# Attention, MLP and gated MLP in one kernel: keys and values in two runs a batch, the shared tile scored once, side work placed anew

## The chip, the cores and the metric

One core of one Trainium2 chip runs the whole kernel. The metric is the device time of one execution in microseconds (us). Everything is in float32; most products are taken as three matmuls over a high and a low part of each operand.

## The reference, cut to what matters

```python
# q, k, v: [8 batches, 8 heads, 576, 64]; phi: [8, 8, 576, 32]
a = phi - max(phi, axis=2); a = exp(a); a = a / (sum(a, axis=2) + 1e-9)
k_m = einsum('bhsm,bhsd->bhmd', a, k)        # 32 memory slots a head
v_m = einsum('bhsm,bhsd->bhmd', a, v)
s = q @ k_m.T / sqrt(64); s = exp(s - max(s)); attn = s / (sum(s) + 1e-9)
x = (attn @ v_m) laid out as [8, 576, 512]
x = x + relu(layer_norm(x) * g_ln @ w_ch1) @ w_ch2          # hidden width 2048
h = gelu(x @ w_in); u, w = halves of h                       # width 1024
out = x + (u * (w_sg @ layer_norm(w) + b_sg)) @ w_out       # w_sg: 576 x 576
```

## The kernel before, in words

Phase 1 is attention and the first MLP. The 8 batches go through it in 4 pairs of an even and an odd batch. A pair has 9 tiles of 128 rows; tile 4, the shared tile, holds the last 64 rows of the even batch and the first 64 of the odd one. Phase 2 is the gated MLP, after all of phase 1.

The MLP's first weight is folded with the values: per batch and per block of 512 hidden columns (fb, four of them), `pvw` = values x centred w_ch1 (16 matmuls, a "vw run", `make_vw`), and the hidden activations come out of the attention weights and `vw` directly: `ph` (line L541), then relu and its low part (`hh` on ACT, `hl` on DVE; `cr` for the 64 columns that belong to the shared tile), then `py` (L570 to L572) sums the second product. `ph` and `py` are the main work of PE (TensorE) in phase 1. A list of steps, one per block of columns and chunk of hidden units, sets their order.

All the rest is side work: for each batch `load_phi`, `prep_max`, `prep_exp`, `prep_sum` (slot weights; `pt`, `mb`, `ptsum` on PE), `load_kv` and `prep_kv` (`kvp`, sums of keys and values over the sequence), `prep_T` (`ptk`, transposed keys), `prep_vb`, and for each group of q tiles `lay_q` and `load_q` (q goes through DRAM, `q_d`), `t_q` (`qT`, a transpose on DVE), `t_scores` (`sc`), `t_norm`, `t_attn`, `t_x` (`px`) and `t_ln`. Each is entered with `at_time(time, ...)`. Times count in units in which a batch's main steps take 18; the list is sorted and the entries are emitted between main steps. `BASES` has the times of a batch's three groups of q tiles, `vw_at` those of the vw runs, and the times around keys and values follow from the batch's first group. A scheduler then orders each engine's instructions by their emission and by what they wait for, and an engine works through its order strictly. So an instruction that waits holds up all behind it on its engine. All loads and stores are issued by SP (L83), in its own order.

Keys and values in detail: a batch has 576 = 4 x 128 + 64 rows. From batch 1 on `prep_kv` runs three times a batch: 32 matmuls over the full chunks of heads 0 to 3, 16 over the 64 remaining rows of all heads (`phir`), 32 over the full chunks of heads 4 to 7. Tile `kv` has two buffers, of which a run takes two, and the remainder takes two of the same tag; so the loads of a run can start only when the run before has read its buffers. Every matmul of a run waits for all loads of the run. DVE then scales (`kvn`, L304) or scales and adds (L307).

Scores and vw runs first have DVE clear two columns of each of the two output buffers (L367, L483); all of a run's matmuls wait for both clears, so a run starts only once DVE has come to them in its order. These outputs, `kvp`, `ptk`, `px` and the small transposes share two PSUM buffers (`ps_a`).

Of the kernel before, what the change touches and what calls it, by code (L numbers as in the profile page):

```python
# [28 lines left out]
def fused_kernel(ctx: ExitStack, tc: tile.TileContext, q, k, v, phi, g1, w1, w2, w_in, g2, w_sg, b_sg, w_out, out):  # L29
# [5 lines left out]
    DM = H * D  # L35
# [26 lines left out]
    ones = const.tile([P, P], F32, name="ones")  # L62
    G.memset(ones, 1.0)
# [74 lines left out]
    def phase1():  # L138
# [32 lines left out]
        def load_phi(b, gs):  # L171
            if gs[0] == 0:
                st["phi", b] = (
                    at.tile([P, H, 4, NM], F32, tag="phi", name="phi"),
                    at.tile([REM, H, NM], F32, tag="phir", name="phir"),
                )
            ph, pr = st["phi", b]
            hs = slice(4 * gs[0], 4 * gs[-1] + 4)
            with behind_w2(b, 5):
                load(ph[:, hs], phi[b, hs, 0:4 * P, :].rearrange("h (p c) m -> p h c m", c=4))  # L180
                load(pr[:, hs], phi[b, hs, 4 * P:S, :].rearrange("h p m -> p h m"))

        def load_kv(b, g, part):
            n = 3 * g + part
# [5 lines left out]
            with behind_w2(b, 6 + n):  # L190
                ins = []
                for i, src in enumerate((k, v)):
                    if part < 2:
                        ld = load(
                            t[:, i],
                            src[b, hs, 0:4 * P, :].rearrange("h (p c) d -> p h c d", c=4)[:, :, 2 * part:2 * part + 2, :],
                        )
                    else:
                        ld = load(t[:REM, i, :, 0, :], src[b, hs, 4 * P:S, :].rearrange("h p d -> p h d"))
                    ins.append(ld.ins.name)  # L200
            st["kv", b, g, part] = t, ins

# [26 lines left out]
        def prep_max(b, gs):  # L229
# [13 lines left out]
            for g in range(n):  # L243
                V.tensor_scalar(dg[:, g, :], ident, mx[:, g:g + 1], None, op0=ALU.mult)
            st["dg", b] = dg

        def prep_exp(b, gs):
# [3 lines left out]
            PE.matmul(mb.rearrange("p h m -> p (h m)"), ones, st["dg", b].rearrange("p g n -> p (g n)"), start=True, stop=True)  # L251
            V.tensor_tensor(out=ph[:, hs], in0=ph[:, hs], in1=mb.unsqueeze(2).to_broadcast([P, 4 * n, 4, NM]), op=ALU.subtract)
            V.tensor_tensor(out=pr[:, hs], in0=pr[:, hs], in1=mb[:REM], op=ALU.subtract)
            A.activation(ph[:, hs], ph[:, hs], AF.Exp)
            A.activation(pr[:, hs], pr[:, hs], AF.Exp)

        def prep_sum(b):
# [5 lines left out]
            G.tensor_tensor(out=sm[:REM], in0=sm[:REM], in1=pr, op=ALU.add)  # L263
# [9 lines left out]
        def prep_kv(b, *parts):  # L273
            ph, pr = st["phi", b]
            if b or parts[0] == (0, 0):
                st["kvp", b] = ps_a.tile([P, 2, 2, D], F32, tag="a", name="kvp")
            if ("kvn", b) not in st:
                st["kvn", b], st["seen", b] = at.tile([P, 2, 2, D], F32, tag="kva", name="kvn"), set()
            kvp, kvn, seen = st["kvp", b], st["kvn", b], st["seen", b]
            kvs = {gp: st.pop(("kv", b, *gp)) for gp in parts}  # L280
            lands = [n for _, ins in kvs.values() for n in ins] if b else []
            for g in sorted({g for g, _ in parts}):
                cs = [c for g_, part in parts if g_ == g for c in range(2 * part, min(2 * part + 2, 5))]
                ts = {part: kvs[g, part][0] for g_, part in parts if g_ == g}
                for c in cs:
                    n = P if c < 4 else REM
                    for j in range(4):
                        h = 4 * g + j
                        mm = PE.matmul(  # L289
                            kvp[32 * j:32 * j + 32, :, g, :],  # L290
                            ph[:, h, c, :] if c < 4 else pr[:, h, :],
                            ts[c // 2][:n, :, j, c % 2, :],
                            start=(c == (cs[0] if b else 0)),
                            stop=(c == (cs[-1] if b else 4)),
                            skip_group_check=True,
                        )
                        for name in lands:
                            tc.add_manual_dep(mm.ins, name, ORDER, reason="all of the group together")
            if not b:
                return  # L300
            rs = st["rs", b]
            for g in sorted({g for g, _ in parts}):
                if g not in seen:
                    V.tensor_scalar(kvn[:, :, g, :], kvp[:, :, g, :], rs[:, g:g + 1], None, op0=ALU.mult)  # L304
                    seen.add(g)
                else:
                    V.scalar_tensor_tensor(  # L307
                        out=kvn[:, :, g, :], in0=kvp[:, :, g, :], scalar=rs[:, g:g + 1], in1=kvn[:, :, g, :], op0=ALU.mult, op1=ALU.add
                    )

        def prep_norm(b):
            kvp, kvn, rs = st["kvp", b], st["kvn", b], st["rs", b]
            for g in range(2):
                V.tensor_scalar(kvn[:, :, g, :], kvp[:, :, g, :], rs[:, g:g + 1], None, op0=ALU.mult)
# [48 lines left out]
        def t_scores(gr):  # L363
            w, b = gr["w"], gr["b"]
            kT, qT = st["kvT", b][0][:, 0, :], gr["qT"]
# [635 lines left out]
```

## Time and profile before

| what | us |
|---|---|
| three timed runs | 1247.18, 1250.12, 1248.4 |
| their median | 1248.4 |
| the profiled execution | 1248.95 |
| its span in the trace | 1247.1 |
| busy time of PE / DVE / ACT / POOL | 1190.5 / 708.1 / 467.1 / 399.0 |

The span is the trace's own extent; the profiled execution's time is 1.85 us more. The granted clock of TensorE is 0.99 of full speed over the span. Phase 1 ends and phase 2's main work begins at about 795 us. In the trace's timelines a row is a start, a length, the engine and line, the operation with its output and inputs, the number of instructions in it, and in brackets the idle time of the engine before it with what ended that; overlapping lengths of pipelined matmuls are normal, so what one costs is read from one start to the next.

### The profile page before, as it was taken

The page shows a single profiled execution, that of the slowest core. Times are in us where ns is not written, and L with a number is a line of the kernel's source. Part 1 is how long each engine was busy: PE and PEld are TensorE (multiplying, and loading weights), DVE is VectorE, ACT ScalarE, POOL GpSimd, SP SyncE. Part 2 cuts the span into 40 slices and gives each one's busy share as a digit, 9 for nine tenths or more (in the row PEclk, how much of TensorE's full clock was granted, in tenths as well). Part 3 has the DMA queues.
Part 4 walks back from the last instruction along what each step waited for, and adds up shares of the span by engine and source line. Part 5 has one row for each costly group of instructions (what it writes and reads, how often), then busy time and mean ns, then how long its engine had stood idle before and what let it go on. Part 6 is the DMA issues. An engine that isn't in the chain of part 4 may idle for free.

```text
span 1247.1 us, 21009 instructions
## 1 busy us (share of the span) xinstructions
PE 1190.5 (95%) x7711; PEld 990.4 (79%) x7711; DVE 708.1 (57%) x1699; ACT 467.1 (37%) x1067; POOL 399.0 (32%) x617
## 2 busy tenths in 40 slices
PE   5699799989999999999999989999999999999998
PEld 3377578877887878878877767789988988998997
DVE  2886564464645654655545566664467457547632
ACT  2665232223333333333323445433354354444430
POOL 2133211121111121111211233324486565657641
PEclk9899999999999999999999999999999999999999
DMA  9996761437515436426353254120141033013201
GB/s 204 266 261 190 215 176 35 145 73 201 119 52 169 109 81 188 94 65 174 89 140 94 68 169 134 51 79 26 51 126 52 1 117 112 1 59 103 77 18 68
DMA packets 204406, 138.85 MB, mean 111 GB/s; under 512 B 94992, under 2 KB 176016, under 8 KB 204304
## 3 DMA queue, kind: packets, MB, share of 16 engines
q1 hardware_dynamic: 204304, 137.51, 40.2%
q8 instruction: 61, 1.00, 0.3%
q14 instruction: 41, 0.34, 0.1%
HBM read 114.40 MB, written 31.33 MB: 117 GB/s over the span
## 4 chain that ended last, share of the span: by engine, by line
PE 79%; DMA 7%; DVE 6%; ACT 2%; issue 2%; SPq 2%; POOL 1%; DVEq 0%; POOLq 0%; ACTq 0%
PE ph L541 13%; PE pvs L910 10%; PE py L570 9%; PE py L571 8%; PE py L572 8%; PE pu L885 8%; PE po L933 8%; PE pv L815 8%; DMA raw<-in_moe_w_ch_dram 3%; PE pvw L487 2%; SPq L83 2%; DMA q<-q_d 2%; PE kvp L289 2%; DMA raw<-in_moe_w_in_dram 1%; DVE qT L358 1%
## 5 line engine op out<-in xcount | busy, mean ns | idle before, releaser
L541 PE MATMUL ph<-aTh,vw 128*128 128x320 f32 (+1 forms) x1024 | 246.3, 301 | 5.3 <-ACT vw L498 3.7
L570 PE MATMUL py<-whl,hh 128*128 128x512 f32 x512 | 206.9, 407 | 6.2 <-ACT hh L527 5.8
L571 PE MATMUL py<-whl,hh 128*128 128x512 f32 x512 | 203.2, 397 | 0.0
L541 PEld LDWEIGHTS ph<-aTh,vw 128*128 128x128 f32 x1024 | 178.4, 191 | 29.3 <-ACT vw L498 9.0
L572 PE MATMUL py<-whl,hl 128*128 128x512 f32 x512 | 183.5, 397 | 0.0
L527 ACT ACTIVATE hh<-ph 128x256 fp32r<-128x256 f32 x256 | 96.3, 384 | 169.3 <-PE ph L541 114.0
L528 DVE SCALAR_TENSOR_TENSOR hl<-ph,hh 128x256 fp32r<-128x256 f32 x256 | 106.1, 419 | 86.8 <-ACT hh L527 85.3
L541 PE MATMUL ph<-aTl,vw 128*128 128x320 f32 (+1 forms) x512 | 153.1, 300 | 0.0
L570 PEld LDWEIGHTS py<-whl,hh 128*128 128x128 f32 x512 | 97.1, 190 | 42.0 <-ACT hh L527 16.8
L910 PE MATMUL pvs<-wsh,vhl 128*128 128x288 f32 x576 | 121.4, 294 | 0.0
L571 PEld LDWEIGHTS py<-whl,hh 128*128 128x128 f32 x512 | 97.4, 190 | 20.9 <-issue 3.1
L885 PE MATMUL pu<-yTh,whl 128*128 128x288 f32 x512 | 111.3, 295 | 0.0
L541 PEld LDWEIGHTS ph<-aTl,vw 128*128 128x128 f32 x512 | 97.6, 191 | 9.8 <-issue 2.1
L572 PEld LDWEIGHTS py<-whl,hl 128*128 128x128 f32 x512 | 90.6, 189 | 12.6 <-issue 3.1
L910 PEld LDWEIGHTS pvs<-wsh,vhl 128*128 128x128 f32 x576 | 94.3, 188 | 0.5
L394 POOL TENSOR_TENSOR z<-z,r 128x512 f32<-128x512 f32 (+1 forms) x21 | 17.5, 833 | 233.6 <-DVE r L393 148.5
L815 PE MATMUL pv<-whl,yTh 128*128 128x512 f32 x288 | 90.9, 395 | 0.0
L933 PE MATMUL po<-whl,gh 128*128 128x512 f32 x288 | 90.3, 391 | 0.0
L885 PEld LDWEIGHTS pu<-yTh,whl 128*128 128x128 f32 x512 | 85.2, 188 | 1.0
L910 PE MATMUL pvs<-wsl,vhl 128*128 128x288 f32 x256 | 75.4, 295 | 0.0
L885 PE MATMUL pu<-yTl,whl 128*128 128x288 f32 x256 | 75.4, 295 | 0.0
L527 ACT ACTIVATE cr<-ph 128x64 fp32r<-128x64 f32 x128 | 28.3, 222 | 122.6 <-PE ph L541 122.4
(156 smaller groups left out, 2218.2 us busy)
## 6 DMA issues: line engine op xcount, KB each, us to landing
wc<-w_d SPq DMA_DIRECT2D x56, 512.0 KB, 5.0
y_d<-x SPq DMA_DIRECT2D x36, 256.0 KB, 2.6
yt<-y_d SPq DMA_DIRECT2D x36, 256.0 KB, 2.7
yr<-y_d SPq DMA_DIRECT2D x36, 256.0 KB, 2.9
kv<-in_k_dram SPq DMA_DIRECT2D x32, 256.0 KB, 4.4
kv<-in_v_dram SPq DMA_DIRECT2D x32, 256.0 KB, 4.5
raw<-in_moe_w_ch_dram SPq DMA_DIRECT2D x32, 256.0 KB, 8.2
raw<-in_moe_w_ch_dram SPq DMA_DIRECT2D x16, 512.0 KB, 7.2
```

Of the source, the lines that this page charges most:

```text
L83: return nc.sync.dma_start(out=out_ap, in_=in_ap)
L289: mm = PE.matmul(kvp[32 * j:32 * j + 32, :, g, :], ph[:, h, c, :] if c < 4 else pr[:, h, :], ts[c // 2][:n, :, j, c % 2, :], start=(c == ( ...
L527: A.activation(out_h, src, AF.Relu)
L528: return V.scalar_tensor_tensor(out=out_l, in0=src, scalar=0.0, in1=out_h.bitcast(F32), op0=ALU.max, op1=ALU.subtract)
L541: PE.matmul(ph, w_[:, ks], x[:, g, 0:w], start=(n == 0), stop=(n == 3 * HK - 1))
L570: PE.matmul(py, hh, wh, start=start, stop=False)
L571: PE.matmul(py, hh, wl, start=False, stop=False)
L572: PE.matmul(py, hl, wh, start=False, stop=stop)
L815: PE.matmul(pv, y[:, kc, cs], w, start=(n == 0), stop=(n == 3 * KC - 1))
L885: PE.matmul(pu, w[:, ds_], y[:, kc, cs], start=(n == 0), stop=(n == 3 * KC - 1))
L910: PE.matmul(pvs, v_, w_, start=(n == 0), stop=(n == len(ops) - 1))
L933: PE.matmul(po, gg[:, dc, cs], w, start=(n == 0), stop=(n == 3 * KC - 1))
```

## The change

- Keys and values: the 64 remaining rows get a tile of their own (`kvr`, heads 0 to 3 on partitions 0 to 63, heads 4 to 7 on 64 to 127, four loads, `load_rem`), and `phir` is laid the same way (two loads for one). `prep_kv(b, g)` is now one run for each half of the heads: 32 matmuls over the chunks and 8 over the remainder, into one sum, and one scaling on DVE in place of two. Its times are 4.4 and 8.4 after `pb` (5.2 and 7.4 in the odd batches from 3 on) in place of 4.4, 6.6 and 8.8; the first run's loads come at `pb`, the second's right behind the first run. Time `pb` stands 11 units (5.5 in batches 1 and 2) ahead of the batch's first group.
- The matrix of ones is dropped: `mb` uses `mean`, and the diagonal is scaled by 512.
- Shared tile: in pairs 1 to 3 its two halves are one group of the odd batch, scored in one run (8 matmuls with either batch's keys), with one chain of softmax. Pair 0 keeps them apart.
- Times: `BASES` has two groups for an even batch and three for an odd one; the odd batch's last group moves from 11.0 (9.5 in pair 3) to 7.2 and the others are set anew. The vw runs of a batch stand 2.2 units apart in place of 2 where the batch's first group sets them, and batch 1's second another 0.7 later; the first one's own time is -10.8 or -10 in place of -12. Loads of q go by the time of the q transpose before them.

```diff
@@ prep_kv @@
-            for g in sorted({g for g, _ in parts}):
-                cs = [c for g_, part in parts if g_ == g for c in range(2 * part, min(2 * part + 2, 5))]
...
+            kvp = ps_a.tile([P, 2, D], F32, tag="a", name="kvp")
+            ts = [st.pop(("kv", b, g, part)) for part in range(2)]
+            lands = [n for t in (*ts, st["kvr", b]) for n in t[1]] if b else []
+            rows = slice(REM * g, REM * g + REM)
+            for c in range(5):
+                for j in range(4):
+                    mm = PE.matmul(
+                        kvp[32 * j:32 * j + 32],
+                        ph[:, 4 * g + j, c, :] if c < 4 else pr[rows, j, :],
+                        ts[c // 2][0][:, :, j, c % 2, :] if c < 4 else st["kvr", b][0][rows, :, j, :],
...
@@ t_scores @@
+            parts = [(st["kvT", b][0][:, 0, :], slice(0, w))]
+            if gr["us"][0]["b"] != b:
+                parts = [(st["kvT", u["b"]][0][:, 0, :], slice(i * n, i * n + n)) for i, u in enumerate(gr["us"])]
...
@@ times @@
         BASES = {
-            0: (None, None, None, 10.0, 11.8, 17.5),
-            1: (-14.0, -8.5, -3.5, 0.5, 4.0, 11.0),
-            2: (-16.0, -9.5, -3.5, 0.5, 4.0, 11.0),
-            3: (-16.0, -9.8, -4.2, -0.8, 2.5, 9.5),
+            0: (None, None, 10.0, 11.8, 17.5),
+            1: (-14.0, -9.5, -0.6, 3.0, 7.2),
+            2: (-16.0, -10.2, -0.6, 3.0, 7.2),
+            3: (-16.0, -10.2, -0.6, 3.0, 7.2),
         }
...
-                for n, gps in enumerate([((0, 0), (0, 1)), ((0, 2), (1, 2)), ((1, 0), (1, 1))]):
-                    at_time(pb + (4.4, 6.6, 8.8)[n] * f, prep_kv, b, *gps)
-                    for i, gp in enumerate(gps):
-                        at_time(pb + (0, 4.5, 6.7)[n] * f + i * (f if n == 0 else 0.01), load_kv, b, *gp)
+            kv_at = (4.0, 6.7) if b == 0 else (5.2, 7.4) if odd and b > 1 else (4.4, 8.4)
+            for g in range(2):
+                at_time(pb + kv_at[g] * f, prep_kv, b, g)
+                for part in range(2):
+                    n = 2 * g + part
+                    at_time(pb - 4 + n if b == 0 else pb + (0.5 * part if g == 0 else kv_at[0] + 0.1 + 0.01 * part) * f, load_kv, b, g, part)
...
-                    vw_at = 18 * b + ((-12, -6.8, -4.2, -1.7) if b % 2 else (-12, -5.3, -3.3, -1.3))[fb]
-                    vw_at = max(vw_at, first + 0.5 + 2 * fb)
+                    vw_at = 18 * b + ((-10.8, -6.8, -4.2, -1.7) if b % 2 else (-10, -5.3, -3.3, -1.3))[fb]
+                    vw_at = max(vw_at, first + 0.5 + 2.2 * fb + 0.7 * (b == 1 and fb == 1))
```

PE in batch 0's main work, where batch 1's keys and values are summed; before (`kvp<-kv,phir` is the remainder, the rows of `py` are main work, `cm` is the column mean of w_ch1's last block, `pvw` that block's vw run for batch 0):

```order
314 L289 MATMUL kvp<-kv,phir 32x2x64 x8
315 L468 MATMUL cm<-wc,mean 128x512 x4
316 L570 MATMUL py_775<-whl,hh 128x512
317 L571 MATMUL py_775<-whl,hh 128x512
318 L572 MATMUL py_775<-whl,hl 128x512
319 L570 MATMUL py_779<-whl,hh 128x512
320 L571 MATMUL py_779<-whl,hh 128x512
321 L572 MATMUL py_779<-whl,hl 128x512
322 L289 MATMUL kvp<-kv,phi 32x2x64 x16
323 L487 MATMUL pvw<-wc,kvT 32x512 x8
324 L541 MATMUL ph<-aTh,vw 128x256
```

The same place after:

```order
291 L577 MATMUL py_621<-whl,hh 128x512
292 L474 MATMUL cm<-wc,mean 128x512 x4
293 L578 MATMUL py_621<-whl,hl 128x512
294 L576 MATMUL py_625<-whl,hh 128x512
...
304 L547 MATMUL ph<-aTl,vw 128x320
305 L547 MATMUL ph<-aTh,vw 128x320
306 L291 MATMUL kvp<-kv,phi 32x128 x16
307 L291 MATMUL kvp<-kvr,phir 32x128 x4
308 L577 MATMUL py_779<-whl,hh 128x512
```

The second half of the heads, with its remainder, now has two steps of main work between `cm` and itself, and the vw run no longer stands right behind it (it comes 21 rows of this order further on).

PE where batch 3's side work begins, before:

```order
912 L266 MATMUL ptsum<-ident,sm 128x128 x2
913 L572 MATMUL py_3120<-whl,hl 128x512
914 L572 MATMUL py_3124<-whl,hl 128x512
915 L371 MATMUL sc<-qT,kvT 32x256 x8
916 L487 MATMUL pvw<-wc,kvT 32x512 x8
917 L541 MATMUL ph<-aTh,vw 128x256
918 L541 MATMUL ph<-aTl,vw 128x256
919 L541 MATMUL ph<-aTh,vw 128x256
920 L541 MATMUL ph<-aTl,vw 128x256
921 L289 MATMUL kvp<-kv,phi 32x2x64 x16
```

After:

```order
812 L577 MATMUL py_2594<-whl,hh 128x512
813 L371 MATMUL sc<-qT,kvT 32x256 x8
814 L547 MATMUL ph<-aTh,vw 128x256
...
835 L577 MATMUL py_2594<-whl,hh 128x512
836 L493 MATMUL pvw<-wc,kvT 32x512 x8
837 L547 MATMUL ph<-aTh,vw 128x256
...
857 L577 MATMUL py_2594<-whl,hh 128x512
858 L291 MATMUL kvp<-kv,phi 32x128 x16
859 L291 MATMUL kvp<-kvr,phir 32x128 x4
860 L427 MATMUL px<-VBh_147,aTl 128x256
861 L428 MATMUL px<-VBl_148,aTh 128x256
```

Before, `ptsum`, `sc`, `pvw` and `kvp` stand within ten rows; after, with some 20 rows of `ph` and `py` between any two (and `ptsum` 19 rows ahead of `sc`).

DVE in the last batch, where phase 2's first rows are read back (`yb` transposes `yt`, loaded from DRAM); before:

```order
940 L89 TENSOR_SCALAR rs_t<-ve 128x2
941 L499 TENSOR_TENSOR vw<-pvw,vw 128x512 x2
942 L792 STREAM_TRANSPOSE yb<-yt 128x512
943 L528 SCALAR_TENSOR_TENSOR cr<-ph,cr 128x64
944 L792 STREAM_TRANSPOSE yb<-yt 128x512
945 L528 SCALAR_TENSOR_TENSOR hl<-ph,hh 128x256 x2
946 L108 TENSOR_SCALAR raw<-raw 128x256
947 L109 SCALAR_TENSOR_TENSOR raw<-raw 128x256
```

After (`raw` is w_in being unpacked, `wsl` the low part of w_sg):

```order
928 L534 SCALAR_TENSOR_TENSOR cr<-ph,cr 128x64
929 L106 TENSOR_SCALAR raw<-raw 128x256
930 L107 SCALAR_TENSOR_TENSOR raw<-raw 128x256
931 L776 TENSOR_TENSOR wsl<-ptw,wsh 128x512
932 L534 SCALAR_TENSOR_TENSOR hl<-ph,hh 128x256
933 L803 STREAM_TRANSPOSE yb<-yt 128x512
934 L534 SCALAR_TENSOR_TENSOR hl<-ph,hh 128x256
935 L803 STREAM_TRANSPOSE yb<-yt 128x512
936 L776 TENSOR_TENSOR wsl<-ptw,wsh 128x64 x2
937 L534 SCALAR_TENSOR_TENSOR cr<-ph,cr 128x64
```

The first `yb` moves behind the unpacking and splitting of the first weights of phase 2, and stands between two `hl`, no longer between a vw split and a `cr`.

## Rows read from the trace of the kernel before

**Rows 1.** Table of stretches: length, busy PE, PEld, DVE, ACT, POOL; granted clock, DMA share, GB/s
```profile
0.00:62.00 62.00, 36.18 (x225) 20.00 (x226) 34.68 (x81) 27.87 (x52) 11.43 (x24) 0.92 0.98 236
...
125.00:170.00 45.00, 36.06 (x277) 23.38 (x276) 29.19 (x70) 13.54 (x34) 8.82 (x11) 0.96 0.75 208
...
262.00:310.00 48.00, 43.40 (x378) 33.50 (x377) 24.33 (x75) 15.28 (x37) 10.92 (x22) 0.96 0.56 152
...
310.00:660.00 350.00, 349.21 (x2469) 285.16 (x2468) 191.40 (x512) 109.24 (x284) 51.95 (x92) 1.00 0.43 116
...
720.00:795.00 75.00, 66.64 (x333) 50.52 (x333) 51.34 (x116) 38.21 (x102) 28.99 (x31) 0.98 0.48 140
...
795.00:1247.00 452.00, 447.88 (x2672) 406.10 (x2670) 251.52 (x533) 177.62 (x351) 243.05 (x375) 1.00 0.21 63
```

**Rows 2.** PE's timeline, 125 to 134 us; start, length, name, count, [idle before <-releaser]
```profile
125.24 0.64 PE L289 MATMUL kvp<-kv,phir 64*32 64x128 f32 x16
125.81 1.55 PE L468 MATMUL cm<-wc,mean 128*128 128x512 f32 x3
...
132.10 1.08 PE L289 MATMUL kvp<-kv,phi 128*32 128x128 f32 x32 [1.20 <-DVE pvw L483]
133.87 1.09 PE L487 MATMUL pvw<-wc,kvT 64*32 64x512 f32 x16 [0.69 <-DVE pvw L483]
```

**Rows 3.** SP's timeline, a load of batch 1 and one of q
```profile
125.73 0.38 SPq L83 DMA_DIRECT2D kv<-in_k_dram  x1
...
147.79 1.76 SPq L83 DMA_DIRECT2D q<-q_d  x4
```

**Rows 4.** PE's timeline, 149 to 168 us
```profile
149.21 0.41 PE L541 MATMUL ph<-aTh,vw 128*128 128x320 f32 x1 [1.38 <-DVE hl L528]
...
156.54 1.96 PE L487 MATMUL pvw<-wc,kvT 64*32 64x512 f32 x16 [2.67 <-issue]
...
167.40 1.09 PE L487 MATMUL pvw<-wc,kvT 64*32 64x512 f32 x16 [0.93 <-DVE pvw L483]
```

**Rows 5.** DVE's timeline in the same stretch
```profile
146.36 1.09 DVE L358 STREAM_TRANSPOSE qT<-q 128x512 f32<-128x512 f32 x1 [2.21 <-DMA q<-q_d]
...
154.76 1.08 DVE L358 STREAM_TRANSPOSE qT<-q 128x512 f32<-128x512 f32 x1 [3.67 <-DMA q<-q_d]
...
165.32 1.96 DVE L235 TENSOR_REDUCE pm<-phi 128x256 f32<-128x1024 f32 x1
```

**Rows 6.** PE's timeline, 271 to 278 us
```profile
271.32 0.67 PE L371 MATMUL sc<-qT,kvT 64*32 64x256 f32 x16 [0.41 <-DVE rs L270]
...
274.00 1.09 PE L487 MATMUL pvw<-wc,kvT 64*32 64x512 f32 x16 [2.01 <-DVE pvw L483]
...
275.83 0.42 PE L541 MATMUL ph<-aTh,vw 128*128 128x256 f32 x1 [0.74 <-ACT vw L498]
...
277.05 1.94 PE L289 MATMUL kvp<-kv,phi 128*32 128x128 f32 x32 [0.16 <-DVE vw L499]
```

**Rows 7.** Table of stretches, 277 to 280 us
```profile
277.00:280.00 3.00, 2.95 (x39) 2.48 (x40) 1.72 (x5) 0.62 (x1) 1.52 (x2) 0.59 0.83 158
```

**Rows 8.** PE's timeline, 722 to 728 us
```profile
722.42 0.41 PE L541 MATMUL ph<-aTh,vw 128*128 128x320 f32 x1 [0.73 <-ACT vw L498]
...
727.42 0.49 PE L572 MATMUL py<-whl,cr 128*128 128x512 f32 x1 [2.02 <-DVE cr L528]
```

**Rows 9.** DVE's timeline at the same place
```profile
726.18 1.08 DVE L792 STREAM_TRANSPOSE yb<-yt 128x512 f32<-128x512 f32 x1 [2.49 <-DMA yt<-y_d]
```

**Rows 10.** PE's timeline, a full run of keys and values and what follows it
```profile
302.17 1.08 PE L289 MATMUL kvp<-kv,phi 128*32 128x128 f32 x32
303.18 0.50 PE L541 MATMUL ph<-aTh,vw 128*128 128x256 f32 x2
```

**Rows 11.** What SP waited for, whole span; in total, times, longest
```profile
SPq L83 <- DVE qT L358: 81.8, 8, 26.0
...
SPq L83 <- PE kvp L289: 39.7, 15, 5.5
```

More of the change, by code (lines that the diff above doesn't have):

```diff
@@ L180, in load_phi @@
                 load(ph[:, hs], phi[b, hs, 0:4 * P, :].rearrange("h (p c) m -> p h c m", c=4))
-                load(pr[:, hs], phi[b, hs, 4 * P:S, :].rearrange("h p m -> p h m"))
+                for g in gs:
+                    load(pr[REM * g:REM * g + REM], phi[b, 4 * g:4 * g + 4, 4 * P:S, :].rearrange("h p m -> p h m"))
         def load_kv(b, g, part):
-            n = 3 * g + part
+            n = 2 * g + part
             if b == 0 and n >= 2:
@@ L262, in prep_sum @@
                 G.tensor_tensor(out=sm, in0=sm, in1=ph[:, :, c, :], op=ALU.add)
-            G.tensor_tensor(out=sm[:REM], in0=sm[:REM], in1=pr, op=ALU.add)
+            for g in range(2):
+                rows, sub = slice(REM * g, REM * g + REM), slice(4 * g, 4 * g + 4)
+                G.tensor_tensor(out=sm[rows, sub], in0=sm[rows, sub], in1=pr[rows], op=ALU.add)
             pt = ps_of(b, [P, 2, P], "ptsum")
@@ L271, in prep_sum, with prep_kv @@
             st["rs", b] = rs
-        def prep_kv(b, *parts):
+        def prep_kv(b, g):
             ph, pr = st["phi", b]
[L275 to L281, printed above, removed]
-            for g in sorted({g for g, _ in parts}):
-                cs = [c for g_, part in parts if g_ == g for c in range(2 * part, min(2 * part + 2, 5))]
[L284 to L308, printed above, removed]
-                    )
@@ L311, in prep_norm @@
[L311 to L314, printed above, removed]
+            kvp = ps_a.tile([P, 2, D], F32, tag="a", name="kvp")
[8 more added lines that the diff above has]
+                        ts[c // 2][0][:, :, j, c % 2, :] if c < 4 else st["kvr", b][0][rows, :, j, :],
+                        start=(c == 0),
+                        stop=(c == 4),
+                        skip_group_check=True,
+                    )
+                    for n in lands:
+                        tc.add_manual_dep(mm.ins, n, ORDER, reason="all of the group together")
@@ L316, in prep_vb, with prep_norm @@
+            if b == 0:
+                st["kvp", g] = kvp
+            else:
+                prep_norm(b, g, kvp)
+        def prep_norm(b, g, kvp=None):
+            if g == 0:
+                st["kvn", b] = at.tile([P, 2, 2, D], F32, tag="kvn", name="kvn")
+            kvn, rs = st["kvn", b], st["rs", b]
+            V.tensor_scalar(kvn[:, :, g, :], st["kvp", g] if kvp is None else kvp, rs[:, g:g + 1], None, op0=ALU.mult)
         def prep_vb(b):
@@ L627, in phase1 @@
             for gi, (items, base) in enumerate(zip(groups, bases)):
[L628 removed]
                 n = REM if items[0][1] == 4 else P
[L630 to L631 removed]
+                gr = {"b": b, "n": n, "w": n * len(items)}
+                gr["us"] = us = []
+                for tt, qi, o, ub in items:
+                    s0 = qi * P if ub % 2 == 0 else 0 if qi == 4 else REM + qi * P
+                    us.append({"seen": set(), "b": ub, "n": n, "o": o, "T": tiles[tt], "at": where(ub, s0)})
                 if b == 0:
[L633 to L634 removed]
+                    for i, (tt, qi, _, ub) in enumerate(items):
+                        at_time(-27, load_q, us[i], ub, qi)
                         at_time(-21 + 0.1 * tt, t_q, gr, i)
```

120 lines of the change are left out of this document (65 added, 55 removed).

## The prediction

> **What bounds the kernel now.** I read the table of stretches first [rows 1]. From 310 to 660 us PE is busy 349.21 of 350 us, and from 795 us to the end 447.88 of 452. There PE's own work is the time: an edit gains there only by taking matmuls away, and can lose by making PE wait. In the first 62 us PE is busy 36.18 us, with a DMA share of 0.98, so the loads set that stretch. What is left are three stretches in which PE idles while side work is squeezed between its main steps: 45.00 - 36.06 = 8.9 us from 125 to 170, 48.00 - 43.40 = 4.6 from 262 to 310, and 75.00 - 66.64 = 8.4 from 720 to 795. The change moves side work in all three, so I then read PE's timeline there, and at each idle gap the timeline of the engine that it names. A gap's bracket names what came last; what stood in that engine's way is in its own timeline.
>
> One more thing is read there: after a gap the granted clock can be low. From 277 to 280 us it is 0.59 of full speed [rows 7], about half way between the levels 1.2 and 2.4 GHz, and a run of 32 matmuls for keys and values that lasts 1.08 us elsewhere [rows 2, 10] lasts 1.94 there [rows 6]. So some gaps cost up to 0.86 us beyond themselves.
>
> **Terms, place by place.** All against the profiled execution, 1248.95 us (span 1247.1 and 1.85 around it); that is 0.55 above the median of 1248.4.
>
> 1. Batch 1's last run of keys and values. The remainder's run starts at 125.24 [rows 2]; the loads for the third run need its buffers and are issued from 125.73 [rows 3], so that run starts at 132.10 after 1.20 us of idle time, and the vw run right behind it after another 0.69 [rows 2]. After, the remainder has a tile of its own, the second run of keys and values follows the first with 18 `ph`, 14 `py` and 4 `cm` matmuls between, about 6.7 us by the pitches in PE's timeline (an estimate), against the 6.4 us from first issue to start that the rows show. The vw run stands 21 rows further on. I take both gaps as gone: -1.9. The cover is thin: if the loads are 1 us slower the term is -0.9, if they fall behind a store that SP must wait for it is +1. Bounds -1.9 to +1.
>
> 2. The gap of 1.38 us at 149.21 [rows 4]. `hl` is late because DVE stands at `qT`, which waits 2.21 us for q [rows 5]; SP issued that load behind keys, values, phi and wc. After, keys, values and phi of batch 2 come earlier in SP's order, the q load's place behind wc is unchanged. I take -1.0; bounds 0 and -1.4.
>
> 3. The vw run at 156.54: 2.67 us idle, then 1.96 us long where others take 1.09 [rows 4], together 3.5. The bracket says "issue", but the clears of its outputs stand in DVE's order behind `qT` at 154.76, which waited 3.67 us for a load issued at 147.79, when the transpose before it (146.36) had given up the only q buffer [rows 3, 5]. After, DVE's order is the same here; but the vw run comes later by about 2.3 us of main work, and the first transpose of the chain earlier by term 2. Most of the gap should close: -2.5, bounds 0 and -3.5.
>
> 4. The vw run at 167.40, 0.93 us [rows 4]: its second clear stands behind the maximum over phi, 1.96 us on DVE [rows 5]. After, the vw spacing changes and that maximum stands behind the clears: -0.9, bounds 0 and -0.9.
>
> 5. Batch 3's start. `sc`, the vw run and the run of keys and values are released within 6 us: gaps of 0.41, 2.01 and 0.16 us and the slow run, 0.86 [rows 6, 7]. The second clear for the vw run waits on DVE behind the transposes of the scores' output, so scores and vw in direct succession always pay. After, about 20 rows of main work stand between any two of them, some 4 us. All but the 0.74 us between a vw run and the next `ph` [rows 6], which is the ACT copy and stays, goes: -3.4, bounds -1 (if `sc` alone is helped) and -3.4.
>
> 6. The gap of 2.02 us at 727.42 [rows 8]: `cr` stands on DVE behind the first `yb`, which waits 2.49 us for the read-back of y [rows 9]. After, the odd batch's last group is done earlier, the first unpacking of w_in stands ahead of `yb`, and the loads of w_sg and w_in ahead of the read-back on SP. -2.0. `yb` will still wait if the read-back is late, and the w_in unpacking can itself hold `cr`: bounds -2.0 and +1.
>
> Sum of the terms: 1.9 + 1.0 + 2.5 + 0.9 + 3.4 + 2.0 = 11.7 us. Ends: all at their best 13.1, all at their worst +1.
>
> **What I cost at nothing.** The runs themselves: 32 matmuls take 303.18 - 302.17 = 1.01 us from start to next start [rows 10], 16 take 125.81 - 125.24 = 0.57 [rows 2], so 0.0275 a matmul and 0.13 a run. A batch pays 2 x 1.01 + 0.57 = 2.59 now. Two runs of 40 would take 2 x 1.23 = 2.46 if the shorter contraction of the remainder may follow inside the run for nothing, and 2 x 1.36 = 2.72 if it costs as much as a run of its own. Over 7 batches that is -0.9 to +0.9. I take 0.
>
> The Trainium skill has a rule that speaks against this part: "Mode switching requires drain" (page "TensorEngine Tiling (Array Packing)", section Key Properties), that is, going from tiles of 128 rows to tiles of 64 within a run empties the array. By it the dearer figure holds and the time would be 0.9 us above my sum; by the cheap reading 0.9 below. No run of before mixes the two shapes, so its trace does not settle it.
>
> The shared tile's scoring in one run takes away three run overheads of 0.13, and half of a chain on DVE and ACT in three pairs, where PE had 0.8 us of idle time in 350 [rows 1]: 0, bounds 0 and -0.5. Where that cover goes, the longer run needs both batches' keys and waits for the later. The dropped matrix, the scaling by 512, one DVE scaling less a run, and one more load issue for phir are hidden behind PE's main work, for the same reason.
>
> **New waits.** Loads of keys and values for the second run now follow the first within some 8 to 12 us in batches 2 to 7. What can be queued ahead of them on SP is a q load that waits for its buffer; such waits add up to 81.8 us in 8, those for keys' buffers to 39.7 in 15, 5.5 at most [rows 11]. What queues behind a late run is all of PE. I allow one such wait of the size seen, 1.20 [rows 2], taken as +1.0. Bounds 0 and 6 batches x (2.4 + 0.86) = 20, below.
>
> So 11.7 - 1.0 = 10.7 off 1248.95, 1238.2, and with the 0.55 to the median about 1238.
>
> **Rivals.**
> - The gaps only move. PE's gaps come from DVE and SP orders that have as many entries as before, and when one wait goes the next one, 0.7 us or so behind it, takes its place: at 132.10, 133.87 three follow each other. Against: the entries are moved 20 rows apart, not swapped. Gain 2.5 us at most: about 1247.
> - Part is realised: the gap of term 3 (the q chain has the same order on DVE), half of term 5 and that of term 6 stay. 10.7 - 2.5 - 1.7 - 2.0 = 4.5: about 1244.
> - More than the sum: the rest of the idle time of 720 to 795 (8.4 less the 2.0 counted) and the slow clock behind each gap go too: 1238 - 6.4 - 3 = about 1229. Against it: what holds PE after 730 is unpacking w_in and transposing y, which is the same work after.
> - Slower: the second runs' loads are late. In batches 2 to 7 the loads for the heads 4 to 7 stand behind q loads on SP, whose buffer is freed by a `qT` that DVE reaches late. If each of the six runs then waits 2.4 us (twice the 1.20 seen in batch 1) and has the slow clock behind it, 0.86, that is 6 x 3.26 = 19.6: about 1257.5. It decides from 10.7 / 6 = 1.8 us a batch on. For it: SP's waits for `qT`, up to 26.0 us [rows 11], and PE's 350 us with no slack. Against: the nearest pair of runs has 6.7 us between, against 6.4 in the rows, and the others have 8 to 12.
>
> **How the numbers follow.** Forecast as summed (1234 to 1241) 0.42; part realised 0.20; more 0.10; only moved 0.14; slower 0.14. 0.2%, 2.5 us, is about what a measurement of this kernel can tell from no change; so faster 0.72, same 0.14, slower 0.14. The likeliest gives 1238. The range leaves out the larger half of the slower case and the better half of the bigger gain: 1229 to 1250. The likeliest case's own range is 1234 to 1241.
>
> **What would show it.** Terms 1 to 4: idle time of PE between 125 and 170 us falls from 8.9 to about 3. Term 5: between 262 and 310 from 4.6 to about 1.5, with a full clock. Term 6: no gap of 2 us with `cr` as its cause near 725. The runs: 40 matmuls in 1.23 to 1.36 us. New waits: gaps before `kvp` in batches 2 to 7 that end with a load of keys or values. The forecast is wrong if 310 to 660 shows more than 3 us of idle time, or if the gap at 156 is still there with its transposed q late.

## The result and the profile after

| | us |
|---|---|
| before, median of 4 runs | 1247.89 (1247.18 to 1250.12) |
| after, median of 4 runs | 1231.63 (1228.96 to 1232.54) |
| ratio after to before, 95% interval | 0.9863 (0.9843 to 0.9883) |
| predicted | 1238 (1229 to 1250) |

The kernel is faster by 1.4%, about 17 us, where 10.7 were forecast. The profiled execution has a span of 1229.5 us against 1247.1.

First the table of stretches of the kernel after, in the columns of [rows 1]:

```profile
125.00:170.00 45.00, 39.45 (x299) 28.29 (x298) 28.15 (x73) 16.26 (x41) 8.90 (x11) 0.96 0.77 205
...
262.00:310.00 48.00, 48.00 (x366) 38.98 (x365) 24.41 (x65) 14.27 (x38) 4.92 (x13) 1.00 0.61 162
310.00:660.00 350.00, 350.00 (x2511) 284.44 (x2510) 184.04 (x494) 109.09 (x287) 54.90 (x99) 1.00 0.42 114
...
720.00:795.00 75.00, 66.92 (x333) 54.25 (x332) 45.72 (x105) 34.98 (x89) 25.47 (x29) 0.98 0.33 100
```

Idle time from 125 to 170 us falls from 8.9 to 45.00 - 39.45 = 5.6 us, and from 262 to 310 from 4.6 to none, at a full clock. From 310 to 660 PE does not idle at all. From 720 to 795 it idles as long as before, 8.1 us, but what is done there is not the same work: the kernel is 14 to 18 us ahead there.

For that reason a second measure is used below, which compares equal work. Take each matmul's time to the start of the next, less the median of that time between matmuls of its kind and shape (over the kernels before and after), and sum it between equal counts of main matmuls (`ph` and `py`). It holds idle time, slow clock and the cost of changing between kinds. Times in the first column are those of the kernel before; e3 to e12 are experiments, below:

| excess in us, main matmuls | before | after | e3 | e5 | e10 | e11 | e12 |
|---|---|---|---|---|---|---|---|
| 0 to 250 (to 118 us) | 44.9 | 44.4 | 43.7 | 47.4 | 47.3 | 46.8 | 45.4 |
| 250 to 400 (to 172) | 18.9 | 15.1 | 18.5 | 16.7 | 15.7 | 17.4 | 12.5 |
| 400 to 1000 (to 311) | 19.9 | 12.7 | 15.4 | 17.3 | 13.0 | 15.8 | 12.7 |
| 1000 to 2600 (to 665) | 35.2 | 34.1 | 44.0 | 36.5 | 34.3 | 37.5 | 34.1 |
| 2600 to 2860 (to 731) | 11.7 | 5.3 | 12.0 | 12.2 | 6.4 | 5.8 | 6.3 |
| 2860 to 3264 (to 837) | 12.6 | 13.8 | 8.8 | 9.6 | 9.3 | 12.5 | 10.4 |
| the rest of phase 2 | 2.1 | 3.1 | 3.1 | 2.1 | 3.1 | 3.1 | 3.1 |
| sum | 145.1 | 128.4 | 145.5 | 141.7 | 129.0 | 138.8 | 124.4 |

The gain of 16.8 us stands in three places: 3.7 in batch 1, 7.2 up to batch 3, 6.4 before phase 2, less 1.2 in the end of phase 1. (Differences in the first and the last row are not read: each column is one execution, and over all the versions below the first 118 us have 42 to 49 us of excess.)

PE's timeline after, at batch 1's second run of keys and values (the place of [rows 2]):

```profile
125.17 1.08 PE L291 MATMUL kvp<-kv,phi 128*32 128x128 f32 x32
...
131.30 1.09 PE L493 MATMUL pvw<-wc,kvT 64*32 64x512 f32 x16
133.15 0.39 PE L547 MATMUL ph<-aTh,vw 128*128 128x256 f32 x1 [0.75 <-ACT vw L504]
```

Both gaps of [rows 2] are gone; the 0.75 us between a vw run and the next `ph` is there still. A little further on, PE, then ACT, then DVE, then SP (the gaps of [rows 4] and the waits of [rows 5]):

```profile
153.43 0.80 PE L576 MATMUL py<-whl,hh 128*128 128x512 f32 x1 [2.70 <-ACT hh L533]
...
157.19 1.09 PE L493 MATMUL pvw<-wc,kvT 64*32 64x512 f32 x16
```

```profile
153.00 0.38 ACT L533 ACTIVATE hh<-ph 128x256 fp32r<-128x256 f32 x1 [4.10 <-DVE cr L534]
```

```profile
150.60 1.08 DVE L354 STREAM_TRANSPOSE qT<-q 128x512 f32<-128x512 f32 x1 [3.36 <-DMA q<-q_d]
```

```profile
142.86 1.09 SPq L81 DMA_DIRECT2D wc<-w_d  x2
143.99 1.82 SPq L81 DMA_DIRECT2D q<-q_d  x4
```

The vw run no longer idles, but the gap has not gone: it stands 4 us ahead of it, at a `py` that waits for `hh`, which ACT gives only when DVE has read the `ph` before it (`cr`), and DVE stands at `qT`, which waits 3.36 us for a load issued at 143.99. So the wait for q of [rows 5] is still there; PE meets it at another instruction.

What moved most is seen on SP and PE at batch 3's preparation: the load of its phi and the transpose of its maximum, before and after.

```profile
225.51 0.51 SPq L83 DMA_DIRECT2D phi<-in_phi_dram  x1
```

```profile
208.28 0.44 SPq L81 DMA_DIRECT2D phi<-in_phi_dram  x1
```

```profile
251.01 0.38 PE L239 MATMUL pt<-ident,pm 128*128 128x128 f32 x2
```

```profile
228.56 0.38 PE L244 MATMUL pt<-ident,pm 128*128 128x128 f32 x2
```

Batch 3's preparation begins 22 us earlier, so it is over when the vw run and the keys of 271 to 278 us [rows 6] come, and these find nothing in their way (no bracket, so no idle time ahead of them; the keys' row is shown in the part on the prediction):

```profile
266.44 1.09 PE L493 MATMUL pvw<-wc,kvT 64*32 64x512 f32 x16
```

The same at the end of phase 1, the first loads of w_in on SP, before and after:

```profile
725.81 1.49 SPq L83 DMA_DIRECT2D raw<-in_moe_w_in_dram  x3
```

```profile
689.06 16.09 SPq L81 DMA_DIRECT2D raw<-in_moe_w_in_dram  x6
```

They are issued 37 us earlier.

### The profile page after: what moved, and what is told of

Same layout as the page of the kernel before. It is cut to its first block, busy times and chain, and to the rows that moved or that the text cites. A ratio compares the mean times of both kernels' runs of the same rounds, so it can differ in the third digit from the quotient of the medians.

```text
span 1229.5 us, 20968 instructions
## 1 busy us (share of the span) xinstructions
PE 1180.5 (96%) x7711; PEld 984.9 (80%) x7711; DVE 694.2 (56%) x1669; ACT 466.5 (38%) x1064; POOL 399.1 (32%) x621
## 4 chain that ended last, share of the span: by engine, by line
PE 81%; DMA 6%; DVE 3%; issue 3%; SPq 3%; ACT 2%; POOL 2%; DVEq 0%; POOLq 0%; ACTq 0%
PE ph L547 14%; PE pvs L921 10%; PE py L576 9%; PE py L578 9%; PE py L577 9%; PE pu L896 8%; PE po L944 8%; PE pv L826 8%; DMA raw<-in_moe_w_ch_dram 3%; SPq L81 3%; PE pvw L493 2%; PE kvp L291 2%; DMA raw<-in_moe_w_in_dram 1%; DMA q<-q_d 1%; DMA raw<-in_moe_w_out_dram 1%
## 5 line engine op out<-in xcount | busy, mean ns | idle before, releaser
L578 PE MATMUL py<-whl,hl 128*128 128x512 f32 x512 | 186.3, 397 | 0.0
L547 PE MATMUL ph<-aTl,vw 128*128 128x256 f32 (+1 forms) x512 | 152.6, 298 | 0.0
L547 PEld LDWEIGHTS ph<-aTl,vw 128*128 128x128 f32 x512 | 97.3, 190 | 10.2 <-issue 2.1
L578 PEld LDWEIGHTS py<-whl,hl 128*128 128x128 f32 x512 | 91.4, 189 | 15.7 <-issue 5.7
L924 POOL TENSOR_TENSOR gt<-gt,ug 128x288 f32<-128x288 f32 x64 | 51.7, 809 | 71.7 <-DVE gt L923 71.6
```

What stands on the lines that cost most here:

```text
L547: PE.matmul(ph, w_[:, ks], x[:, g, 0:w], start=(n == 0), stop=(n == 3 * HK - 1))
L578: PE.matmul(py, hl, wh, start=False, stop=stop)
L924: G.tensor_tensor(out=gt, in0=gt, in1=ug, op=ALU.mult)
```

## The experiments

All ratios are to the kernel before, run on the same chip beside it, over 4 to 12 runs of the version; the bracket is the 95% interval.

**e1: two of the new times in the kernel before.**

```diff
-            at_time(pb + (2.6 if b else 6) * f, prep_sum, b)
+            at_time(pb + (1.6 if b else 6) * f, prep_sum, b)
-            1: (-14.0, -8.5, -3.5, 0.5, 4.0, 11.0),
+            1: (-14.0, -9.5, -3.5, 0.5, 4.0, 11.0),
```

> The kernel before with two of the new times alone: the second q group of batch 2 one unit earlier (-8.5 to -9.5) and ptsum one unit earlier (2.6 to 1.6). Theory: what the changed kernel won between 170 and 310 us (7.2 us of PE's pitch beyond the normal one) came from ptsum, scores, vw run and keys and values no longer standing in succession, so these two numbers alone give back 5 to 7 us, 1241 to 1243, and PE's idle time from 262 to 310 us falls from 4.6 to under 1. Rival: the two-run form of keys and values with its new times made the room; then under 2 us, 1246 or more, and at least 2.5 us of that idle time stay.

0.9998 (0.9984 to 1.0012). PE's timeline shows the same two gaps as [rows 6]:

```profile
272.60 0.67 PE L371 MATMUL sc<-qT,kvT 64*32 64x256 f32 x16 [0.41 <-DVE rs L270]
275.28 1.09 PE L487 MATMUL pvw<-wc,kvT 64*32 64x512 f32 x16 [2.01 <-DVE pvw L483]
```

The theory falls for these two times. An entry's time sets when it is emitted, not when its input is there: `ptsum` waits for phi, whose load stands about where it stood (227.03 us; 225.51 before), so `sc` and the vw run still follow it at once.

**e2: the last group of batch 7 at 7.2 in the kernel before.** (`-0.8, 2.5, 9.5` becomes `-0.8, 2.5, 7.2`.)

> The kernel before with one number changed: the last q group of batch 7 at 7.2 in place of 9.5. Theory: the 6.4 us that the changed kernel won from 665 to 730 us came from this group alone (its chain and the vw run behind it stood against the read-back of y), so 1242 to 1243 and no gap with cr near 725. Rival: the group shares DVE with everything else of batch 7, and the gain needs the merged shared tile too, which takes a chain out of there; then under 3 us, 1245 or more.

1.0001 (0.9987 to 1.0016). The gap with `cr` is gone, and another stands in its place. PE, then DVE:

```profile
723.71 0.63 PE L755 MATMUL ptw<-ident,ws 128*128 128x128 f32 x4 [1.99 <-DMA ws<-in_moe_w_sg_dram]
```

```profile
725.32 0.30 DVE L108 TENSOR_SCALAR raw<-raw 128x256 uint32<-128x256 uint32 x1 [3.19 <-DMA raw<-in_moe_w_in_dram]
```

SP had the stores of y (718 us) ahead of the loads of w_sg and w_in as before; now DVE waits 3.19 us for w_in where it waited 2.49 for y [rows 9]. The wait was turned into another.

**e3: the changed kernel with three runs of keys and values.** Everything of the changed kernel but its key and value part (loads, `prep_kv`, their times), which is the old one.

> The changed kernel with keys and values in three runs a batch again, at the old offsets from pb, all else as changed. Theory: the two-run form is worth only batch 1's gap (1.2 + 0.7 us, and the slow clock behind it, about 1), and costs 0.13 us in each of 6 batches since the run of 40 takes 1.36, so +2 to +3, 1233.5 to 1235, with a gap before kvp near 130 us back. Rival: the two runs are what frees PE and DVE all through phase 1; then +6 us or more, 1238.

1.0015 (1.0002 to 1.0029), 1251.81 us: the whole gain is gone, so the rival is nearer, and worse than it said. PE's timeline, the gap of [rows 2] and two of the three longest between 125 and 800 us (behind these, 2.77 us at 157 and 2.26 at 781):

```profile
131.04 1.08 PE L289 MATMUL kvp<-kv,phi 128*32 128x128 f32 x32 [1.26 <-DVE pvw L493]
...
309.85 0.56 PE L551 MATMUL ph<-aTh,vw 128*128 128x320 f32 x2 [3.01 <-ACT aTh L414]
...
679.38 0.56 PE L551 MATMUL ph<-aTh,vw 128*128 128x320 f32 x2 [3.08 <-ACT aTh L414]
```

The first is [rows 2] again. The other two, and a like one of 3.01 us at 493.33, are the shared tile of each pair: scored in one run, it needs the odd batch's keys, which the third run brings too late. In the table these gaps make 1000 to 2600 dearer than before (44.0) and are 3.1 of the 12.0 us before phase 2; from 400 to 1000, where none of the three lies, 4.5 of the change's 7.2 us are won with three runs. So this run prices the new times and the merged tile without early keys. Three runs with the new times and the halves apart were not run, and what the two runs alone give is e5's question.

**e4: two buffers for q.**

```diff
-                t = at.tile([P, 4 * DM // 16, 4], F32, tag="q", name="q")...
+                t = at.tile([P, 4 * DM // 16, 4], F32, tag="q", name="q", bufs=2)...
-                T["x"] = mo.tile([P, DM], F32, tag="x", name="x", bufs=7)
+                T["x"] = mo.tile([P, DM], F32, tag="x", name="x", bufs=6)
```

> The changed kernel with two buffers for q in phase 1 in place of one (and six for x in place of seven, to make room). Theory: the 2.70 us gap at 153 us, and the qT waits of 3.36 and 2.15 us behind it, come from the single q buffer, whose load is issued only after the transpose before; with two they go, 1227 to 1229, and idle time from 125 to 170 us falls from 5.55 to about 2. Rival: the landing takes as long because the transfers beside it (wc, q through DRAM) fill the queues, so q is as late: within 1 us of 1231.6; or six x buffers hold up px, slower.

0.9956 (0.9942 to 0.9969), slower than the changed kernel by about 1%. SP's and PE's timelines:

```profile
148.82 0.89 SPq L81 DMA_DIRECT2D wc<-w_d  x2
149.75 1.36 SPq L81 DMA_DIRECT2D q<-q_d  x3
```

```profile
158.89 0.69 PE L576 MATMUL py<-whl,hh 128*128 128x512 f32 x1 [2.89 <-ACT hh L533]
...
713.40 1.96 PE L493 MATMUL pvw<-wc,kvT 64*32 64x512 f32 x16 [4.43 <-DVE pvw L489]
720.38 1.96 PE L493 MATMUL pvw<-wc,kvT 64*32 64x512 f32 x16 [5.02 <-issue]
```

The gap of 2.9 us stays: the load is still issued only at 149.75, behind wc. Ahead of both, SP stands from 141.97 to 145.49 us at a write of q to DRAM (`q_d`), which waits for the q load before it to land; so q's buffer was not the only thing in its way. The loss is at 713 and 720 us, in stretches where x buffers are in use; that the sixth buffer causes it was not tried apart. For the single buffer the run settles nothing.

**e5: two runs of keys and values alone.** The kernel before with the key and value part of the changed one; groups, shared tile and vw times old.

> The kernel before with keys and values in two runs a batch alone (own tile for the remainder, their new times around pb), all other times and the two halves of the shared tile as before. Theory: the third run held the only phi tile and the buffers, so phi of the next batch came late (17 us later in batch 3) and its side work ran into that of the batch before it; two runs alone give 8 to 11 us, 1237 to 1240, and the idle time of PE from 262 to 310 us (4.6 us) goes. Rival: the loss of 20 us with three runs came from the shared tile scored once, which needs the odd batch's keys early; then two runs are worth only batch 1's gap, 2 to 3 us, 1245 or more.

0.9958 (0.9940 to 0.9976), 5 us: between the two. The gaps of [rows 2] are gone, and 2.6 us of excess up to batch 3, but the 6.4 before phase 2 are not (12.2 in the table).

**e6: the shared tile's halves apart.** In the changed kernel: `[[hi], ...]` for the odd batch, `[[lo]]` in the even one at -3.5 (-4.2 in pair 3), the odd half at 0.2 so that its batch's preparation keeps its time.

> The changed kernel with the shared tile's halves scored apart again in pairs 1 to 3 (the even batch's half at its old times, the odd one's one unit before keys and values need it), all else as changed. Theory: scoring them together saves three runs and half a chain that are hidden, so 0 to 2 us, 1231.5 to 1233.5. Rival: the chain taken off DVE and the sole q and z tiles is what makes the last group's earlier place possible; then 4 us or more, 1235.5 or more, lost between 665 and 800 us.

0.9859 (0.9840 to 0.9877): no difference from the changed kernel, as the theory said. In the changed kernel with its two runs the merged scoring is worth nothing.

**e7: the last group of batch 7 back at 9.5 in the changed kernel.** (`7.2` becomes `9.5` in pair 3.)

> The changed kernel with the last q group of batch 7 back at 9.5 in place of 7.2. Theory: w_in and w_sg are loaded into memory that attention gives back, so an earlier last group is what brings these loads forward (690 us in place of 721); put back, the gap near 725 returns and most of the 6.4 us of that stretch, 1235.5 to 1238. Rival: the rest of batch 7 has been moved forward anyway; within 1.5 us of 1231.6.

0.9837 (0.9817 to 0.9857). The theory falls: put back, the group costs nothing, and may win 0.2% (the intervals overlap). The stretch before phase 2 has 5.2 us of excess, as in the changed kernel (5.3).

**e8: the old times of the vw runs in the changed kernel.**

```diff
-                    vw_at = 18 * b + ((-10.8, -6.8, -4.2, -1.7) if b % 2 else (-10, -5.3, -3.3, -1.3))[fb]
-                    vw_at = max(vw_at, first + 0.5 + 2.2 * fb + 0.7 * (b == 1 and fb == 1))
+                    vw_at = 18 * b + ((-12, -6.8, -4.2, -1.7) if b % 2 else (-12, -5.3, -3.3, -1.3))[fb]
+                    vw_at = max(vw_at, first + 0.5 + 2 * fb)
```

> The changed kernel with the vw runs' old times (-12 for the first, 2 units apart, batch 1's second not moved). Theory: they count in batch 1 alone, where three vw runs, the q chain and keys and values stand close; 1 to 3 us between 125 and 170, 1232.5 to 1234.5. Rival: an earlier first vw run takes a buffer of wc and of vw from the batch before in every batch, 5 us or more; or no difference, within 1 us.

0.9874 (0.9855 to 0.9892): within the noise of the changed kernel.

**e9, e10, e11: which group times.** All have two runs, halves apart, old vw and `ptsum` times, and the changed kernel's rule for q's loads (a load is entered no earlier than the q transpose before it), which e5 has not. e10 has the even batches' new times (second group at -9.5 or -10.2, and `first = bases[0] + 2.0` in place of 1.2, which puts all their preparation 0.8 units later) with the odd ones' old, e11 the odd batches' new times with the even ones' old, e9 the even ones' and the odd ones' but for the last group.

> Two runs a batch and the new times of the q groups alone (even batches' second group at -9.5 or -10.2 and their preparation 0.8 units later; odd batches' groups at 0.2 and 3.0 in place of 0.5 and 4.0, in pair 3 of -0.8 and 2.5); halves apart, old vw times, old ptsum time, last group at 11 or 9.5. Theory: keys done early and groups moved forward need each other; together they are the whole change, so a ratio to before of 0.986 to 0.989 where the two runs alone had 0.9958 and the times with three runs 1.0015. Rival: the small edits (ptsum, vw) carry the rest; then 0.992 or more.

> As the run before, with the odd batches' groups at their old times (0.5, 4.0, 11.0; in pair 3 -0.8, 2.5, 9.5), so two runs a batch and the even batches' new times. Theory: what frees the loads of keys and values from standing behind a q load that waits is the odd batches' earlier second group, so most of the gain beyond two runs is gone here, 0.993 to 0.996, and the gap near 725 us is back. Rival: the even batches' later preparation does it; then 0.988 or less.

> Two runs a batch, the odd batches' new times (0.2, 3.0, 7.2), the even batches' old ones (-8.5, -9.5, -9.8 for the second group, preparation as before); halves apart, old vw and ptsum times. Theory (odd times): 0.986 to 0.989. Rival (even times): 0.993 to 0.996.

e9: 0.9923 (0.9906 to 0.9939). e10: 0.9862 (0.9846 to 0.9879). e11: 0.9940 (0.9926 to 0.9955). The theory (odd times) falls and its rival holds: two runs and the even batches' times, with the rule for q's loads, give all of the change's gain. The odd times add nothing to two runs that the time tells (e11 and e5 overlap), and in e9 they take some of the gain back: 39.9 us of excess from 1000 to 2600, where e10 has 34.3; a gap of 2.90 us at 325 that e10 has not is part of it. The rule for q's loads was not run apart; e11 has it too, so it is not the gain by itself.

One stretch of e11 bears on the prediction's term 6: with odd times and two runs the excess before phase 2 falls from e5's 12.2 to 5.8 (the first loads of w_in come at 697.99, in e5 at 724.37), and e11 loses about half of that again in the end of phase 1 (12.5 us, in e5 9.6).

Why later preparation brings everything forward is seen where e5 and e10 part. PE, DVE and SP of e5 (SP's columns as in [rows 3]):

```profile
197.35 0.27 PE L276 MATMUL ptsum<-ident,sm 128*128 128x128 f32 x1
...
202.42 0.66 PE L367 MATMUL sc<-qT,kvT 64*32 64x256 f32 x16
...
207.19 1.08 PE L291 MATMUL kvp<-kv,phi 128*32 128x128 f32 x32
```

```profile
197.66 0.42 DVE L278 TENSOR_REDUCE rs<-ptsum 128x2 f32<-128x256 f32 x1 [0.21 <-PE ptsum L276]
...
198.50 0.06 DVE L363 MEMSET sc<- 128x2 f32 x1
```

```profile
171.60 7.21 SPq L81 DMA_DIRECT2D wc<-w_d  x4
204.98 1.71 SPq L81 DMA_DIRECT2D q<-q_d  x4
...
209.26 0.55 SPq L81 DMA_DIRECT2D kv<-in_k_dram  x1
```

PE and SP of e10:

```profile
194.16 0.66 PE L371 MATMUL sc<-qT,kvT 64*32 64x256 f32 x16
...
198.92 0.38 PE L276 MATMUL ptsum<-ident,sm 128*128 128x128 f32 x2
...
199.47 1.08 PE L291 MATMUL kvp<-kv,phi 128*32 128x128 f32 x32
```

```profile
171.35 7.20 SPq L81 DMA_DIRECT2D wc<-w_d  x4
196.69 1.72 SPq L81 DMA_DIRECT2D q<-q_d  x4
...
200.46 0.55 SPq L81 DMA_DIRECT2D kv<-in_k_dram  x1
```

In e5's order batch 2's `ptsum` stands ahead of batch 1's last scores. Both use the two PSUM buffers: the second clear for the scores (198.50) comes on DVE behind the reading of `ptsum` (197.66), and `ptsum` needs sums that POOL ends at about 193.5. The scores come at 202.42, the next `qT` on DVE after them, and the q load, which waits for that `qT`, at 204.98. SP stands at it from 179 on, 26.1 us (like the longest wait of [rows 11]), and the loads of keys and values stand behind it, in SP's order. In e10 the preparation is 0.8 units later, the scores come first, 8 us earlier, the q load at 196.69 after a wait of 18.1 us, keys and values at 200.46, and phi of batch 3 at 211.91 in place of 220.84 (225.51 before). e11 has e10's rule for q's loads and differs from it here by the even batches' times (and enters batch 3's preparation 0.3 units earlier, not later), and it does as e5: `ptsum` at 196.95, scores at 202.59, the q load at 205.15, phi at 219.12. So here the even batches' times decide, not the rule for q's loads.

Over all the versions the excess from 400 to 1000 goes with this phi load: 18.3 to 20.0 us where it is issued at 223 to 227 us (before, e1, e2), 15.4 to 17.3 at 218 to 221 (e3, e5, e11), 12.7 to 13.0 at 212.4 or earlier (the changed kernel and all the others with two runs and even times). Two runs alone bring it to 220.84, the new times with three runs to 218.40, both to 211.91 and less: each edit does a part.

**e12: q's load ahead of wc's in batch 1,** with the last group of batch 7 at 9.5.

```diff
-                    at_time(vw_at - (4 if fb == 0 else 2.5), load_wc, fb)
+                    at_time(vw_at - (4 if fb == 0 else 1.2 if b == 1 else 2.5), load_wc, fb)
```

> The changed kernel with the last group of batch 7 back at 9.5 (0.9837 of before when run so) and, in batch 1, the loads of wc for vw runs 1.3 units later, so that q's load stands ahead of wc's 1 MB on SP. Theory: the gap at 153 us (2.7 to 3.2 us) is the q load landing 6.5 us after its issue because wc's transfer is in the way; with q ahead it lands 2 to 3 us earlier and the gap falls under 1 us, 0.981 to 0.983. Rival: the landing is as long as it is, or wc is then late for its vw run: gap the same size or a new one at the vw run, 0.984 or more.

0.9819 (0.9802 to 0.9836), 1227.1 us, the fastest version run, and its interval lies below that of the changed kernel. From e7 it differs by wc's loads alone; there the ratio was 0.9837 and the intervals overlap, so what this edit gives is read at its place. SP, DVE and PE:

```profile
144.18 1.84 SPq L81 DMA_DIRECT2D q<-q_d  x4
146.12 0.84 SPq L81 DMA_DIRECT2D wc<-w_d  x2
```

```profile
148.27 1.06 DVE L354 STREAM_TRANSPOSE qT<-q 128x512 f32<-128x512 f32 x1
...
155.68 1.09 DVE L354 STREAM_TRANSPOSE qT<-q 128x512 f32<-128x512 f32 x1 [2.50 <-DMA q<-q_d]
```

```profile
157.63 0.73 PE L578 MATMUL py<-whl,hl 128*128 128x512 f32 x2 [1.37 <-DVE hl L534]
```

The first q is there when DVE comes to it, at most 2.3 us after its last issue (144.18 + 1.84), where with wc's 1 MB ahead it took 150.60 - 145.81 = 4.8. The gap falls from 2.7 (3.19 in e7) to 1.37 and not under 1, since the q load after that still makes DVE wait 2.50 us. The excess of the stretch falls from 15.1 (15.8 in e7) to 12.5.

## Why the prediction was right, and where it was not

The direction, and the time within its range, came out; 1231.6 is faster than the likeliest case's own range of 1234 to 1241. That it is so near is in part luck: a gap counted as closed stayed, a wait that was added did not come, and two stretches gave about twice or three times their terms for a reason that the sum does not hold. By its steps:

- Term 1 (-1.9, batch 1's run of keys and values): right, and from the cause named. With three runs it is back (e3: 1.26), with two it goes (e5). The cover was not thin: 9.5 us of PE's work lie between the two runs (115.67 to 125.17), not 6.7; the `cm` matmuls there are 8, not 4.
- Term 2 (-1.0) and term 4 (-0.9): both gaps are gone in the profile after. The first nearly goes with the two runs (0.30 us of 1.38 is left in e5), the second with the even batches' times (0.94 us in e5 and e11, none in e10).
- Term 3 (-2.5) failed at "Most of the gap should close". DVE's order is the same, and so is the wait, 3.36 us where it was 3.67; the vw run's later place only let another instruction meet it. By the prediction's own sign (the gap still there, its transposed q late) this step was wrong. About half of the gap comes from the load of wc ahead of q's (e12 leaves 1.37 us). Of the 6.3 us of terms 1 to 4, 3.7 came, and idle time from 125 to 170 us fell to 5.6, not to about 3.
- Term 5 (-3.4) was right in what would be seen, no gap and a full clock from 262 to 310, but it read the distances from the changed order and did not ask what makes them. Two of the new times do not (e1); the excess goes with the phi load, which comes 17 us earlier. Mis-sized: the stretch gave 7.2 us, since the other side work from 172 to 311 us came free with it.
- Term 6 (-2.0) was right that the gap goes, and mis-sized: the stretch gave 6.4 us, less 1.2 after it. Its cause, "the odd batch's last group is done earlier", is neither needed nor enough: with the group put back the stretch stays cheap (e7), and with three runs the earlier group wins nothing (e2). With two runs the even batches' times bring the loads of w_in forward and the excess down (e10: 6.4), and so do the odd ones, that group among them (e11: 5.8). Which of the odd times does it was not tried.
- The runs, taken at 0 with 0.9 on either side: the dear end is right. PE's timeline after, a run of 40:

```profile
272.09 1.08 PE L291 MATMUL kvp<-kv,phi 128*32 128x128 f32 x32
273.10 0.42 PE L291 MATMUL kvp<-kvr,phir 64*32 64x128 f32 x8
273.45 0.39 PE L547 MATMUL ph<-aTh,vw 128*128 128x256 f32 x1
```

273.45 - 272.09 = 1.36 us, in each of the 12 runs of batches 2 to 7, so 0.13 more a batch than three runs. The Trainium skill's "Mode switching requires drain" (page "TensorEngine Tiling (Array Packing)", section Key Properties) spoke for this end; the measured number agrees with it. The prediction's sentence that no run of before mixes the two shapes was false. In batch 0 the kernel before does:

```profile
17.00 1.08 PE L289 MATMUL kvp<-kv,phi 128*32 128x128 f32 x16 [1.31 <-DMA kv<-in_v_dram]
18.01 0.65 PE L289 MATMUL kvp<-kv,phir 64*32 64x128 f32 x8
```

By the starts of the single matmuls each four take 0.21 us here (a slower pace than in the later runs), and from the last four of 128 rows to the first of 64 it is 0.37; so this trace spoke for the dear end.

- New waits, +1.0: none came. PE has no gap before `kvp` from batch 1 on. The slower rival had the right mechanism at the wrong place: a q load that waits at the head of SP with keys and values behind it was a cost of the kernel before, and the change shortened the longest such wait from 26.0 to 18.1 us. The row for it stood in [rows 11] and was used against the change only. The waits did not go away: SP's total for them after is no smaller than the 81.8 us of before, so what counts is which loads stand behind one, not the sum:

```profile
SPq L81 <- DVE qT L354: 86.3, 10, 18.1
```

- 310 to 660 us: 0 was forecast, -1.1 came.
- One sentence was loose: a clock of 0.59 is not half way between the two levels (that is 0.75), but nearer the lower.

So the forecast's sum was too small because it went gap by gap, and each gap's price was the gap alone. What joins them in the rows above is one queue: the preparation ahead of the scores on PE, the scores ahead of `qT`, `qT` ahead of the q load, the q load ahead of keys, values and phi on SP. It is shown at one place, for batch 3's phi. That the loads of later batches come forward by the same queue is argued, not shown, and which of the even batches' two new times (group or preparation) does it was not tried apart.

## What to carry to other kernels

Where one engine issues all loads, look for the load that waits at its head for a buffer, and for what frees that buffer: a step moved later in emission can bring everything behind that load forward. A gap that the trace puts down to one instruction often stays when this instruction is moved; ask what the engine behind it waits for, and whether that wait is gone. And two edits can be worth more together than alone: two runs gave 0.4% (e5); with the even batches' times and the rule for q's loads it was 1.4% (e10), and the phi load came forward by more than two runs (e5) or the new times with three runs (e3) had brought it. Test the pair before dropping either.

## What the runs showed of the hardware

A run of 32 matmuls on 128 rows and 8 on 64 rows takes 1.36 us, where 40 at 0.0275 and one overhead of 0.13 would be 1.23: the change of shape inside the run costs as much as a run's own overhead. The first 32 take 273.10 - 272.09 = 1.01 us, as a run of 32 by itself does [rows 10]. Four q loads of 64 KB were there at most 2.3 us after their last issue, or 4.8 us after it with two loads of 512 KB ahead of them. The slow clock behind the gap of batch 1 falls on what comes next. In the kernel after it is the main matmuls behind 153.43:

```profile
153.40:157.00 3.60, 3.57 (x12) 3.02 (x12) 2.90 (x9) 1.65 (x4) 0.00 (x0) 0.60 0.78 198
157.00:159.00 2.00, 2.00 (x21) 0.85 (x20) 0.55 (x1) 0.06 (x1) 0.00 (x0) 1.00 0.70 144
```

0.60 of full speed for 3.6 us, and 1.00 when the vw run comes (1.09 us); in the kernel before the vw run itself was next and took 1.96 [rows 4]. So a gap moved is not a gap cheaper.
